# The opening of a fused linear-attention and tanh-shrink kernel: lam as eight numbers, other load queues, another order of the first steps

## The chip, the cores and the metric

The kernel runs on one core of a Trainium2 chip. The metric is the device time of one execution in microseconds (us). Beside it stand the times of one profiled execution and its trace.

## The reference

Two stages follow each other. The first is a linear attention with decay over 4 batches, 8 heads, 768 positions and 64 columns per head. The reference goes through blocks of 64 positions:

```python
pos = np.arange(block)
rel = pos[:, None] - pos[None, :]
Dmask = np.where(rel >= 0, lam[:, None, None] ** rel[None, :, :], 0.0)
lam_pow = lam[:, None, None] ** (pos[None, :, None] + 1)
for b in range(nb):
    intra = np.einsum('bhic,bhjc->bhij', qb, kb) * Dmask[None]
    intra = np.einsum('bhij,bhjd->bhid', intra, vb)
    inter = np.einsum('bhid,bhde->bhie', qb * lam_pow[None], kv_state)
    out[:, :, sl] = intra + inter
    kb_dec = kb * (lam[:, None, None] ** (block - 1 - pos[None, :, None]))[None]
    kv_state = lam_block[None, :, None, None] * kv_state + np.einsum('bhsd,bhse->bhde', kb_dec, vb)
```

`lam` holds eight numbers, one for each head. The output, seen as 3072 tokens of 512 numbers, goes into the second stage: `h = x @ w_in` (512 x 2048), `g = h - tanh(h)`, and `g @ w_out` (2048 x 512). `w_in` and `w_out` come as 64-bit floats, seen as 64-bit integers; q, k, v and lam are 32-bit floats.

## The kernel before

The positions are cut into 6 groups of 128, and one group of all 4 batches is 512 tokens. Group 0 is done with plain products; later groups use products of sums (a Strassen-like scheme), which the change does not touch. A chunk is one of q, k or v for one group and one batch: 128 positions x 8 heads x 64 columns, 256 KB, in pieces of 256 bytes.

**The opening steps of group 0.** For each batch b:

- `att_transpose(0, (b,))`: 4 transposes of q and 4 of k on TensorE into PSUM tiles `tp` (L384), each group of four copied out by ScalarE to `qt` and `kt` (L386).
- `att_scores(0, (b,))`: 8 products `sp` (L400), then two VectorE multiplications with the decay table `whole` (L407) to `ss`.
- `att_decay(0, b)`: VectorE multiplies the k chunk by the last column of the table (L430).
- `first_out(b)`: 8 products `op` of v and `ss` (L451). Two batches share a pair of PSUM banks; `first_tokens(half)` copies them to the tokens `xt` by ScalarE (L458).
- `kv_products(0, (b, b+1))`: 16 products `kv` of k and v for two batches (L439); `first_state` copies the result out (L463).

The decay table is made by `scans`: 8 VectorE scans (L110), one for each head, that multiply step by step by that head's lam. They read `lam_all`, a tile of 128 rows that all hold the eight lams, and the identity matrix `ident`, which GpSimd makes. Before, one DMA from GpSimd's queue fills `lam_all` with 128 copies of the eight numbers (L96).

**The plain products of unit 0.** `up_plain(0, ...)` is a generator: each `steps(unit, n)` takes n of its steps. One step is two products `h` (L895) of one block row i of `w_in` with a token tile. The first eight steps are for columns 11 and 21 (the first two batches), the next eight for 12 and 22. At the end of a column ScalarE takes the tanh (L900) and VectorE the difference (L901).

**The weights.** A block of `w_in` is 128 rows x 512 columns, 512 KB as it comes. `load_weights` loads blocks into four buffers `raw64` (WAHEAD = 4) and `weights(n)` rounds blocks until n are done: three ScalarE passes (L332 to L334) and two VectorE passes (L336, L337). Before, the first 16 blocks are all loaded from SP's queue (L260); blocks 2 and 3 of a unit come as two DMAs of 64 rows each (L250).

**What sets the order.** A scheduler orders the instructions on each engine; those given to `keep_in_program_order` (in group 0 nearly all of the opening) stay in the order of the text. `held(op, engines)` makes the next load that each named queue issues wait for `op`. The queues: SP (`nc.sync`) takes q chunks and w_in blocks; ScalarE's queue takes the k chunks of batches 0 and 1; GpSimd's (POOL's) takes v of group 0 and k of batches 2 and 3. An engine's queue issues in order, so a load that waits holds up all behind it.

**Idle products.** `idle_products(n)` puts n products of a tile of zeros into an unused bank (L361); they compute nothing that is read. Eight of them come first, as soon as VectorE has set the zeros (L95).

The text from L966 on lists the opening in order. After it `powers()`, group 1's attention, the other units and the sums follow in the same way as after the change.

Of the kernel before, what the change touches and what calls it, by code (L numbers as in the profile page):

```python
# [9 lines left out]
F32 = mybir.dt.float32  # L10
# [8 lines left out]
BLK = 128  # L19
# [5 lines left out]
def kernel(  # L25
# [32 lines left out]
    nc = tc.nc  # L58
    B, H, S, D = q.shape
# [33 lines left out]
    lam_all = const.tile([128, H], F32)  # L93
    fwd = const.tile([128, NP, BLK], F32)
    nc.vector.memset(fwd[:, 0, :], 0.0)  # L95
    nc.gpsimd.dma_start(out=lam_all, in_=bass.AP(tensor=lam.tensor, offset=lam.offset, ap=[[0, 128], [1, H]]))  # L96
    make_identity(nc, ident)

# [3 lines left out]
    whole = xpool.tile([128, 3, 2, HB], F32, name="whole", tag="tt").rearrange("s a b c -> s (a b c)")[:, 0:2 * DM].rearrange(  # L104
        "s (j p i) -> s j p i", j=2, p=NP)
    def scans(ps, ones):
        for j in range(2):
            for p in ps:
                h = 2 * p + j
                tc.keep_in_program_order(nc.vector.tensor_tensor_scan(  # L110
                    out=whole[:, j, p, :], data0=lam_all[:, h:h + 1].to_broadcast([128, BLK]), data1=ones, initial=0.0,
                    op0=AL.mult, op1=AL.add))


    scans(range(NP), ident)

    def masks():
        pin = tc.keep_in_program_order
# [20 lines left out]
    def tied(yes, op):  # L139
        return tc.keep_in_program_order(op) if yes else op  # L140
# [12 lines left out]
    def load_natural(g, b, names):  # L153
        for name, src, bufs in (("q", q, 2), ("k", k, 3), ("v", v, 4)):
            if name in names:
                if (g, b, name) in ((0, 2, "q"), (0, 3, "q"), (0, 3, "k")):
                    x = opool.tile([128, H, D], F32, name=f"{name}_nat", tag="o")
                else:
                    x = (qpool if name == "q" else io).tile([128, H, D], F32, name=f"{name}_nat", tag=name, bufs=bufs)
                rows = src[b, :, ts(g, BLK), :].rearrange("h s d -> s h d")  # L160
                if name == "q":
                    parts = [(nc.sync, x, rows)]
                elif g == 0:
                    parts = [(nc.scalar if name == "k" and b < 2 else nc.gpsimd, x, rows)]
                else:
                    parts = [(nc.sync, x[ts(1 - t, HALF), 4:8], rows[ts(t, HALF), 4:8]) for t in range(2)]
                    parts.insert(0, (nc.sync, x[:, 0:4], rows[:, 0:4]))
                for eng, to, of in parts:
                    op = tc.keep_in_program_order(eng.dma_start(out=to, in_=of))  # L169
                    if begin.get(eng) is not None:  # L170
                        wait_for(op, begin.pop(eng))
                raw[g, b][name] = x
# [67 lines left out]
    def load_block(eng, dst, kind, n, m, first=False):  # L240

        if kind == "out":
            tied(first, eng.dma_start(out=dst, in_=moe_w_out[ts(m * KH + n, 128), :].rearrange("k (a n) -> k a n", a=2)))
        elif m < 2:
            op = tied(first, eng.dma_start(out=dst, in_=w_in_u[ts(m, 128), :, ts(n, 256)]))
            if begin.get(eng) is not None:
                wait_for(op, begin.pop(eng))
        else:
            for j in range(2):
                op = tied(first, eng.dma_start(out=dst[ts(1 - j, 64)], in_=w_in_u[ts(2 * m + j, 64), :, ts(n, 256)]))  # L250
                if begin.get(eng) is not None:
                    wait_for(op, begin.pop(eng))

    def load_weights(n):

        while ready["loaded"] < min(n, ready["may"]):
            if moe_w_in.dtype != F32:
                raw64 = stage.tile([128, 2, 256], I64, name="raw64", tag="raw64", bufs=WAHEAD)
                block = blocks[ready["loaded"]]
                load_block(nc.gpsimd if ready["loaded"] in range(NU * KI, NU * KI + 4) else nc.sync, raw64, *block, True)  # L260
                wraw[ready["loaded"]] = raw64
            ready["loaded"] += 1

# [75 lines left out]
    def bank(name, tag, bufs):  # L339
        return psum.tile([128, 512], F32, name=name, tag=tag, bufs=bufs)  # L340


    for b in range(B):
        raw[0, b] = {}
    for b in (0, 1):
        load_natural(0, b, "qk")
    ready["may"] = 1
    load_weights(1)
    for b in (0, 1):
        load_natural(0, b, "v")  # L350
    ready["may"] = 2
    load_weights(2)
    at["loaded"] = B


    idle = bank("idle", "w", 1)

    def idle_products(n, first=False):

        for _ in range(n):  # L360
            tied(not first, nc.tensor.matmul(out=idle[:, 0:128], lhsT=fwd[:, 0, :], rhs=fwd[:, 0, :], start=True, stop=True))  # L361

    idle_products(8, True)


    state = const.tile([128, B, NP, D], F32)
# [4 lines left out]
    def att_transpose(g, bs):  # L371
        for b in bs:
            load(g * B + b + 1)
            t = raw[g, b]
            qt = work.tile([128, NP, BLK], F32, name="qt", tag="qt")
            kt = work.tile([128, NP, BLK], F32, name="kt", tag="kt")
            for dst, x in ((qt, "q"), (kt, "k")):
                if g >= GB:
                    tc.keep_in_program_order(nc.vector.transpose(out=dst.rearrange("d p i -> d (p i)"),
                                                                 in_=t[x + "b"].rearrange("d p r a -> d (p r a)")))  # L380
                else:
                    tp = bank("tp", "att", 4).rearrange("d (p s) -> d p s", p=NP)
                    for p in range(NP):
                        tied(g == 0 or p == 0, nc.tensor.transpose(out=tp[:, p, :], in_=t[x][:, 2 * p:2 * p + 2, :],  # L384
                                                                   identity=ident))
                    tied(g == 0, nc.scalar.activation(dst, tp, AF.Copy))  # L386
            qd = None
            if g > 0:
                qd = work.tile([128, NP, BLK], F32, name="qd", tag="qd")
                nc.vector.tensor_tensor(qd, qt, fwd, op=AL.mult)  # L390
            tr[g, b] = (qt, kt, qd)
# [36 lines left out]
    def att_decay(g, b):  # L428
        kp = raw[g, b]["k"].rearrange("s (p j) d -> s p j d", j=2)
        return tied(g != 1, nc.vector.tensor_tensor(kp, kp, bwd if g > 0 else bwd_first, op=AL.mult))  # L430
# [13 lines left out]
    def first_out(b):  # L444
        n, half = b % 2, b // 2
        if n == 0:
            reads[0, half] = [bank("op", "att", 4).rearrange("d (p b s) -> d p b s", p=2, b=2) for _ in range(2)]
        ops, ss, vn = reads[0, half], sc.pop((0, b)), raw[0, b]["v"]
        for p in range(NP):
            for j in range(2):  # L450
                tied(True, nc.tensor.matmul(out=out_dst(ops, n, p, j), lhsT=vn[:, 2 * p + j, :], rhs=ss[:, j, p, :],  # L451
                                            start=n == 0 and p % 2 == 0, stop=n == 1 and p % 2 == 1,
                                            skip_group_check=True))
# [502 lines left out]
    def steps(it, n):  # L956
        for _ in range(n):
            next(it)


    def held(op, *engines):
        begin.clear()
        begin.update({eng: op for eng in engines})

    def more_raw(n):
        ready["may"] = n  # L966
        load_weights(n)

    att_transpose(0, (0,))
    idle_products(3)  # L970
    held(att_scores(0, (0,)), nc.sync, nc.gpsimd)
    load_natural(0, 2, "qk")
    att_decay(0, 0)
    att_transpose(0, (1,))
    idle_products(2)
    first_out(0)
    att_decay(0, 1)
    held(att_scores(0, (1,)), nc.sync)
    more_raw(3)
    kv = kv_products(0, (0, 1))  # L980
    idle_products(2)
    weights(1)
    first_out(1)
    held(first_tokens(0)[0], nc.sync, nc.gpsimd)
    load_natural(0, 3, "qk")
    load_natural(0, 2, "v")
    more_raw(4)
    load_natural(0, 3, "v")
    ready["may"] = len(blocks)
    idle_products(6)  # L990
    unit = up_plain(0, [(i, c + 10 * a) for c in (11, 12) for i in range(KI) for a in range(2)])
    steps(unit, 2)
    weights(2)
    idle_products(4)
    att_transpose(0, (2,))
    steps(unit, 2)
    weights(3)
    att_scores(0, (2,))
    att_decay(0, 2)
    idle_products(6)  # L1000
    att_transpose(0, (3,))
    steps(unit, 2)
    weights(4)
    att_scores(0, (3,))
    first_out(2)
    att_decay(0, 3)
    idle_products(4)
    first_out(3)
    first_tokens(1)
    first_state((0, 1), kv)  # L1010
    steps(unit, 2)
    weights(5)
    steps(unit, 4)
    first_state((2, 3), kv_products(0, (2, 3)))
    weights(6)
    every(unit)
    weights(2 * KI)
# [177 lines left out]
```

## Time and profile before

| what | value |
|---|---|
| median of 3 runs | 657.41 us (657.17 to 658.46) |
| the profiled execution's own time | 657.46 us |
| its span (first to last instruction) | 655.7 us |
| TensorE (PE) busy | 649.3 us, 99% |
| VectorE (DVE) busy | 470.2 us, 72% |
| ScalarE (ACT) busy | 244.3 us, 37% |
| GpSimd (POOL) busy | 206.0 us, 31% |
| granted TensorE clock | 1.00 |

A row of a timeline gives the start and length in us from the span's start, the engine, the line of the kernel, the operation, the tiles written and read, the shape, and how many records were merged. A product of 32-bit floats is two matmul records. In square brackets stands the time for which the engine had been idle, and what ended that idle time. Records of TensorE overlap, so a row's length can reach past the next row's start. A DMA row's length is the time of issuing, not of the transfer. POOLq, SPq and ACTq are the queues' sequencers; in the views of DMA queues, q1 is SP's queue, q10 ScalarE's and q0 POOL's, with packets, MB, and the time of the packets as a share of the 16 DMA engines in that window.

### The profile page before, as it was taken

The numbers are of one execution on the slowest core, as the hardware profiler recorded it, in microseconds if no ns is written. First come the engines' busy times: TensorE is split into PE (matmuls) and PEld (weight loads), VectorE is DVE, ScalarE is ACT, GpSimd is POOL, SyncE is SP. The second block draws the span as 40 slices with busy tenths as digits, with TensorE's granted clock in tenths as the row PEclk, the third lists the DMA queues.
The fourth block names the chain that finished last, engine by engine and source line by source line (L and its number), as shares of the span: only waits on it lengthen the run. The fifth ranks groups of instructions, "written<-read, shape, count | busy, mean of one in ns | idle before, by whom it ended". The sixth has DMA issues, their size and how long they took to land.

```text
span 655.7 us, 14869 instructions
## 1 busy us (share of the span) xinstructions
PE 649.3 (99%) x5782; PEld 595.9 (91%) x5782; DVE 470.2 (72%) x893; ACT 244.3 (37%) x485; POOL 206.0 (31%) x354
## 2 busy tenths in 40 slices
PE   8999999999999999999999999999999999999998
PEld 7888888888888999988999988999988899998897
DVE  4447989968878895678786668788468697466663
ACT  3576964622321223532223442213453223263210
POOL 2100125776133334202335302243411254400241
PEclk9999999999999999999999999999999999999999
DMA  7939977997858768957656967576867476621374
GB/s 194 246 113 214 240 227 209 387 277 222 183 129 218 219 190 246 217 103 184 198 182 219 240 127 161 149 235 196 208 158 153 123 259 219 228 69 33 85 250 163
DMA packets 154422, 125.78 MB, mean 192 GB/s; under 512 B 124928, under 2 KB 127232, under 8 KB 154352
## 3 DMA queue, kind: packets, MB, share of 16 engines
q0 software_dynamic: 27072, 88.04, 43.3%
q1 hardware_dynamic: 125200, 36.27, 25.6%
q8 instruction: 46, 0.75, 0.5%
q10 hardware_dynamic: 2080, 0.52, 0.4%
q14 instruction: 24, 0.20, 0.1%
HBM read 103.81 MB, written 20.97 MB: 190 GB/s over the span
## 4 chain that ended last, share of the span: by engine, by line
PE 80%; DMA 6%; issue 5%; SPq 4%; DVE 3%; POOL 1%; ACT 0%; POOLq 0%; DVEq 0%
PE y L601 14%; PE y L839 12%; PE zw L839 9%; PE h L895 7%; PE y L685 5%; PE z L601 5%; PE acc L925 4%; PE y L786 4%; PE w L786 4%; PE z L685 3%; SPq L181 2%; DMA q_blk<-in_q_dram 2%; SPq L169 2%; PE w L685 1%; PE sp L418 1%
## 5 line engine op out<-in xcount | busy, mean ns | idle before, releaser
L744 POOL DMA_DIRECT2D wb<-fine x148 | 79.9, 540 | 186.3 <-PE y L786 69.6
L843 ACT ACTIVATE q<-y 128x128 f32<-128x128 f32 x96 | 26.7, 278 | 142.8 <-PE y L839 141.9
L839 PE MATMUL y<-wb,g 128*128 128x128 f32 x456 | 60.2, 277 | 0.0
L895 PE MATMUL h<-xt,w 128*128 128x256 f32 x256 | 58.2, 383 | 0.3 <-DVE w L337 0.3
L839 PEld LDWEIGHTS y<-wb,g 128*128 128x128 f32 x456 | 55.1, 192 | 0.6
L895 PEld LDWEIGHTS h<-xt,w 128*128 128x128 f32 x256 | 47.4, 190 | 7.8 <-DVE w L337 1.3
L747 POOL DMA_DIRECT2D wb<-factors x44 | 23.7, 541 | 84.3 <-PE y L786 50.8
L609 ACT ACTIVATE th<-g 128x512 f32<-128x512 f32 x40 | 25.2, 630 | 66.5 <-DVE g L627 50.7
L601 PE MATMUL y<-xt,w 128*128 128x256 f32 x192 | 45.0, 379 | 0.0
L610 DVE TENSOR_TENSOR g<-g,th 128x512 f32<-128x512 f32 x40 | 27.6, 691 | 20.7 <-ACT th L609 20.7
L601 PEld LDWEIGHTS y<-xt,w 128*128 128x128 f32 x192 | 36.4, 190 | 5.1 <-ACT g L618 0.2
L839 PE MATMUL zw<-wb,g 128*128 128x128 f32 x304 | 40.3, 276 | 0.3 <-DMA wb<-fine 0.3
L601 PE MATMUL y<-tt,ws 128*128 128x256 f32 x160 | 37.8, 379 | 0.0
L601 PE MATMUL y<-tt,w 128*128 128x256 f32 x160 | 37.8, 379 | 0.0
L601 PE MATMUL z<-xt,ws 128*128 128x256 f32 x160 | 37.8, 379 | 0.0
L839 PEld LDWEIGHTS zw<-wb,g 128*128 128x128 f32 x304 | 37.0, 192 | 0.7 <-DVE tt L666 0.5
L786 PE MATMUL y<-wb,g 128*128 128x256 f32 x160 | 37.3, 379 | 0.0
L786 PE MATMUL w<-wb,g 128*128 128x256 f32 x160 | 35.3, 379 | 0.0
L786 PEld LDWEIGHTS y<-wb,g 128*128 128x128 f32 x160 | 30.4, 190 | 4.1
L786 PEld LDWEIGHTS w<-wb,g 128*128 128x128 f32 x160 | 30.4, 190 | 4.1
L601 PEld LDWEIGHTS z<-xt,ws 128*128 128x128 f32 x160 | 30.4, 190 | 4.1
L601 PEld LDWEIGHTS y<-tt,w 128*128 128x128 f32 x160 | 30.3, 190 | 4.2
(212 smaller groups left out, 1465.7 us busy)
## 6 DMA issues: line engine op xcount, KB each, us to landing
wb<-fine POOLq DMA_DIRECT2D x148, 256.0 KB, 3.6
wb<-factors POOLq DMA_DIRECT2D x44, 256.0 KB, 4.9
wb<-fine_in POOLq DMA_DIRECT2D x36, 256.0 KB, 4.1
raw<-in_moe_w_out_dram SPq DMA_DIRECT2D x12, 512.0 KB, 5.0
rest<-fine POOLq DMA_DIRECT2D x20, 256.0 KB, 4.3
raw<-in_moe_w_in_dram SPq DMA_DIRECT2D x8, 512.0 KB, 7.2
raw<-in_moe_w_in_dram SPq DMA_DIRECT2D x16, 256.0 KB, 6.2
fine<-f POOLq DMA_DIRECT2D x16, 256.0 KB, 4.8
```

The lines of the kernel that those rows point to most:

```text
L169: op = tc.keep_in_program_order(eng.dma_start(out=to, in_=of))
L601: nc.tensor.matmul(out=t[:, m, :], lhsT=wt[:, kt, ts(m, 128)], rhs=x[:, kt, :], start=first and m == 0 and kt == 0, stop=kt == 1, skip_gro ...
L609: nc.scalar.activation(th, src, AF.Tanh)
L610: nc.vector.tensor_tensor(dst(c), src, th, op=AL.subtract)
L685: nc.tensor.matmul(out=dst[:, ts(u, 128)], lhsT=a, rhs=b, start=x in (1, 2, 5) and u == 0, stop=True, skip_group_check=True)
L744: nc.gpsimd.dma_start(out=t.rearrange("p m c -> p (m c)"), in_=fine[TWICE.index(n_), SUB.index(x_)].rearrange("p u c -> p (u c)"))
L747: nc.gpsimd.dma_start(out=t, in_=factors[XAT[FACT[n_][1]]][:, 2 * x_:2 * x_ + 2, :])
L786: nc.tensor.matmul(out=t[:, m, :], lhsT=a[:, u, kt, ts(m, 128)], rhs=wb[:, kt, :], start=first and u == 0 and m == 0 and kt == 0, stop=u = ...
L839: tied(x == STEPS[-1], nc.tensor.matmul(out=dst, lhsT=a[:, u, :], rhs=wb[:, ts(u, 128)], start=x in (1, 2) and u == 0, stop=u == NU - 1, s ...
L843: nc.scalar.activation(keep, dst, AF.Copy)
L895: tied(u == 0, nc.tensor.matmul(out=hm[c][:, m, :], lhsT=w1[u][:, i, a, ts(m, 128)], rhs=xt[0, t][:, i, :], start=m == 0 and i == 0, stop= ...
L925: nc.tensor.matmul(out=acc[n][:, r, :], lhsT=a[:, ts(r, 128)], rhs=b, start=kt == 0 and r == 0, stop=kt == KH - 1, skip_group_check=True)
```

## The change

- lam is loaded as eight numbers in eight rows (`few`), spread by VectorE to 8 x 128, turned by one small TensorE transpose (`rows`) and copied by VectorE to `lam_all`. The first 8 idle products and this transpose now stand ahead of all other TensorE work.
- v chunks of batches 0 and 1 move from POOL's queue to SP's. The first w_in block moves from SP's queue to POOL's, where it waits for the first scan. k of batch 2 follows it there; v of batch 2 and all of batch 3's k and v follow, held until the first batch's scores.
- q chunks of batches 2 and 3 and w_in blocks 1 to 3 are issued on SP without holds.
- batch 1's transposes and scores come ahead of batch 0's outputs, batch 2's transposes ahead of the first step of `h`; the state products of batches 0 and 1 come later, and the outputs of batches 2 and 3 come between steps of `h`.
- after the first eight, 16 idle products stand where there were 27.

```diff
--- before.py
+++ after.py
@@ -93,8 +93,18 @@
     lam_all = const.tile([128, H], F32)
     fwd = const.tile([128, NP, BLK], F32)
     nc.vector.memset(fwd[:, 0, :], 0.0)
-    nc.gpsimd.dma_start(out=lam_all, in_=bass.AP(tensor=lam.tensor, offset=lam.offset, ap=[[0, 128], [1, H]]))
+    few = const.tile([H, 1], F32, name="few")
+    nc.gpsimd.dma_start(out=few, in_=bass.AP(tensor=lam.tensor, offset=lam.offset, ap=[[1, H], [1, 1]]))
     make_identity(nc, ident)
+
+    idle = psum.tile([128, 512], F32, name="idle", tag="w", bufs=1)
+
+    def idle_products(n, first=False):
+
+        for _ in range(n):
+            op = nc.tensor.matmul(out=idle[:, 0:128], lhsT=fwd[:, 0, :], rhs=fwd[:, 0, :], start=True, stop=True)
+            if not first:
+                tc.keep_in_program_order(op)
 
 
 
@@ -104,15 +114,26 @@
     whole = xpool.tile([128, 3, 2, HB], F32, name="whole", tag="tt").rearrange("s a b c -> s (a b c)")[:, 0:2 * DM].rearrange(
         "s (j p i) -> s j p i", j=2, p=NP)
     def scans(ps, ones):
+        first = None
         for j in range(2):
             for p in ps:
                 h = 2 * p + j
-                tc.keep_in_program_order(nc.vector.tensor_tensor_scan(
+                op = tc.keep_in_program_order(nc.vector.tensor_tensor_scan(
                     out=whole[:, j, p, :], data0=lam_all[:, h:h + 1].to_broadcast([128, BLK]), data1=ones, initial=0.0,
                     op0=AL.mult, op1=AL.add))
-
-
-    scans(range(NP), ident)
+                first = first or op
+        return first
+
+
+    few_wide = xpool.tile([H, BLK], F32, name="few_wide", tag="xt1")
+    tc.keep_in_program_order(nc.vector.tensor_copy(few_wide, few.to_broadcast([H, BLK])))
+    rows = psum.tile([128, 512], F32, name="rows", tag="z", bufs=1)[:, 0:H]
+    idle_products(8, True)
+    tc.keep_in_program_order(nc.tensor.transpose(out=rows, in_=few_wide, identity=ident[0:H, 0:H]))
+    tc.keep_in_program_order(nc.vector.tensor_copy(lam_all, rows))
+
+
+    begun = scans(range(NP), ident)
 
     def masks():
         pin = tc.keep_in_program_order
@@ -161,7 +182,7 @@
                 if name == "q":
                     parts = [(nc.sync, x, rows)]
                 elif g == 0:
-                    parts = [(nc.scalar if name == "k" and b < 2 else nc.gpsimd, x, rows)]
+                    parts = [(nc.gpsimd if b > 1 else nc.scalar if name == "k" else nc.sync, x, rows)]
                 else:
                     parts = [(nc.sync, x[ts(1 - t, HALF), 4:8], rows[ts(t, HALF), 4:8]) for t in range(2)]
                     parts.insert(0, (nc.sync, x[:, 0:4], rows[:, 0:4]))
@@ -257,7 +278,7 @@
             if moe_w_in.dtype != F32:
                 raw64 = stage.tile([128, 2, 256], I64, name="raw64", tag="raw64", bufs=WAHEAD)
                 block = blocks[ready["loaded"]]
-                load_block(nc.gpsimd if ready["loaded"] in range(NU * KI, NU * KI + 4) else nc.sync, raw64, *block, True)
+                load_block(nc.gpsimd if ready["loaded"] in (0, *range(NU * KI, NU * KI + 4)) else nc.sync, raw64, *block, True)
                 wraw[ready["loaded"]] = raw64
             ready["loaded"] += 1
 
@@ -342,25 +363,12 @@
 
     for b in range(B):
         raw[0, b] = {}
-    for b in (0, 1):
-        load_natural(0, b, "qk")
-    ready["may"] = 1
-    load_weights(1)
-    for b in (0, 1):
-        load_natural(0, b, "v")
-    ready["may"] = 2
-    load_weights(2)
+    for names in ("qk", "v"):
+        for b in (0, 1):
+            load_natural(0, b, names)
     at["loaded"] = B
 
 
-    idle = bank("idle", "w", 1)
-
-    def idle_products(n, first=False):
-
-        for _ in range(n):
-            tied(not first, nc.tensor.matmul(out=idle[:, 0:128], lhsT=fwd[:, 0, :], rhs=fwd[:, 0, :], start=True, stop=True))
-
-    idle_products(8, True)
 
 
     state = const.tile([128, B, NP, D], F32)
@@ -966,52 +974,54 @@
         ready["may"] = n
         load_weights(n)
 
+    held(begun, nc.gpsimd)
+    more_raw(1)
+    more_raw(2)
+    load_natural(0, 2, "q")
+    more_raw(3)
+    load_natural(0, 2, "k")
     att_transpose(0, (0,))
-    idle_products(3)
-    held(att_scores(0, (0,)), nc.sync, nc.gpsimd)
-    load_natural(0, 2, "qk")
+    idle_products(4)
+    held(att_scores(0, (0,)), nc.gpsimd)
+    load_natural(0, 2, "v")
+    load_natural(0, 3, "qkv")
+    more_raw(4)
+    ready["may"] = len(blocks)
     att_decay(0, 0)
+    idle_products(1)
     att_transpose(0, (1,))
+    idle_products(4)
+    att_scores(0, (1,))
+    first_out(0)
+    weights(1)
+    att_decay(0, 1)
+    idle_products(5)
+    first_out(1)
+    first_tokens(0)
     idle_products(2)
-    first_out(0)
-    att_decay(0, 1)
-    held(att_scores(0, (1,)), nc.sync)
-    more_raw(3)
-    kv = kv_products(0, (0, 1))
-    idle_products(2)
-    weights(1)
-    first_out(1)
-    held(first_tokens(0)[0], nc.sync, nc.gpsimd)
-    load_natural(0, 3, "qk")
-    load_natural(0, 2, "v")
-    more_raw(4)
-    load_natural(0, 3, "v")
-    ready["may"] = len(blocks)
-    idle_products(6)
+    att_transpose(0, (2,))
+    weights(2)
     unit = up_plain(0, [(i, c + 10 * a) for c in (11, 12) for i in range(KI) for a in range(2)])
     steps(unit, 2)
-    weights(2)
-    idle_products(4)
-    att_transpose(0, (2,))
-    steps(unit, 2)
+    att_scores(0, (2,))
+    kv = kv_products(0, (0, 1))
     weights(3)
-    att_scores(0, (2,))
     att_decay(0, 2)
-    idle_products(6)
     att_transpose(0, (3,))
     steps(unit, 2)
+    first_out(2)
     weights(4)
     att_scores(0, (3,))
-    first_out(2)
     att_decay(0, 3)
-    idle_products(4)
+    steps(unit, 2)
     first_out(3)
     first_tokens(1)
     first_state((0, 1), kv)
     steps(unit, 2)
     weights(5)
-    steps(unit, 4)
+    steps(unit, 2)
     first_state((2, 3), kv_products(0, (2, 3)))
+    steps(unit, 2)
     weights(6)
     every(unit)
     weights(2 * KI)
```

## The prediction, made before the run

> **What bounds the kernel now.** I read the page first, then the timeline of each engine over the first 60 us, the DMA view in short windows, and the chain of waits. The page says that TensorE is the bound:
>
> ```profile
> PE 649.3 (99%) x5782; PEld 595.9 (91%) x5782; DVE 470.2 (72%) x893; ACT 244.3 (37%) x485; POOL 206.0 (31%) x354
> ```
>
> PE is idle for 655.7 - 649.3 = 6.4 us. But some of its "busy" time is idle products, which compute nothing. The timeline of PE (start, length, line, tile, records, idle before) shows where both lie:
>
> ```profile
> 1.06 3.78 PE L361 MATMUL idle<-fwd 128*128 128x128 f32 x16 [1.06 <-DVE fwd L95]
> 4.63 1.08 PE L384 MATMUL tp<-ident,q_nat 128*128 128x128 f32 x4
> ...
> 11.36 1.09 PE L451 MATMUL op<-ss,v_nat 128*64 128x128 f32 x16 [0.67 <-DMA v_nat<-in_v_dram]
> ...
> 16.22 1.60 PE L361 MATMUL idle<-fwd 128*128 128x128 f32 x12
> 17.66 1.89 PE L895 MATMUL h<-xt,w 128*128 128x256 f32 x8
> ...
> 32.44 5.45 PE L895 MATMUL h<-xt,w 128*128 128x256 f32 x24
> ```
>
> Two records make one product, and one h step too is two products. From 32.44 on PE is dense (its only wait up to 60 us is 0.26 us). Everything the change touches lies before that, so I measure it at one mark: the start of the second half of unit 0 (columns 12 and 22), 8 records into the last row, at 32.44 + 1.73 = 34.2 us. What is gained at this mark is gained at the end if nothing later is late.
>
> The two things that came late were lam and v:
>
> ```profile
> 7.09 2.63 DVE L110 TENSOR_TENSOR_SCAN whole<-lam_all,ident 128x128 f32<-128x128 f32 x8 [6.08 <-DMA lam_all<-in_lam_dram]
> 9.64 1.26 DVE L407 TENSOR_TENSOR ss<-sp,whole 128x512 f32<-128x512 f32 x2
> ```
>
> lam was issued at 1.25 and landed 5.7 us later, at 6.95; scans, first scores and first outputs queue behind it. v's first chunk, issued by POOL at 2.44, landed 8.8 us later, at 11.2. The DMA view shows why: by windows of half a microsecond, POOL's queue (q0) moved nothing at 7.0 to 7.5 (first two rows) and 20 packets at 8.0 to 8.5 (last row), though v had been issued by 4.25:
>
> ```profile
> q1 hardware_dynamic: 108, 0.13, 87.2%
> q10 hardware_dynamic: 87, 0.02, 19.5%
> ...
> q0 software_dynamic: 20, 0.08, 41.3%
> ```
>
> While SP's and ACT's queues hold small-packet chunks of q and k, POOL's queue hardly moves; beside the large packets of w_in it gets about half.
>
> **Step prices, from the rows (warm).** Eight transposes of one batch (tp) 0.88 (20.28 to 21.16), scores (sp) 1.09, outputs (op) 1.02, state products of two batches (kv) 1.08, two h steps 1.73, an idle product 0.24 (1.44 us for 6). Work up to the mark: 4 tp + 4 sp + 4 op + kv + 8 h steps = 3.5 + 4.4 + 4.1 + 1.1 + 6.9 = 20.0. So 34.2 - 20.0 = 14.2 us of the opening are waits, idle products, and slow clock.
>
> **Idle products.** The first 8 stay. After them there were 3+2+2+6+4+6+4 = 27, now 4+1+4+5+2 = 16: 11 x 0.24 = 2.6 us of PE less. This is only gain where the operands are there.
>
> **lam.** The DMA of 128 rows becomes one of 8 numbers; added are a DVE copy (8x128, at most the memset's 0.17), one small transpose on PE (a record, about 0.2 to 0.4) and a DVE copy of 128x8 (about 0.1): 0.5 us from landing to the next PE step, 0.8 to the first scan. The new cost is that the small transpose stands in PE's order *ahead of* the first q transposes. These began at 4.63; now they begin at s = landing + 0.5, and everything on PE is queued behind that wait. No row shows an 8-number DMA from POOL; bounds are 4.9 (POOL's packets of lam first moved in the window 4.0 to 4.5, plus receipt) and 7.5 (lam's own 6.95 and some more). I take 6.2: nearest to lam, as the queues ahead are the same (q, k on SP and ACT, same issue times), with less to write and read. So s = 6.7. That is 2.1 us of PE lost at the front, while the scans run from 7.0 to 9.7, as before.
>
> **Clock.** The first products ran at 3.57 / 16 = 0.22 us a record against 0.12 later, and PE was fast only from about 6.7 on, 5.6 us after its first product. Now PE stands idle from 4.84 to 6.7, so I price tp and the 4 idle products behind it as slow ones: tp 1.73 (4.63 to 6.36) for 0.88, and 8 records x 0.22 = 1.78 for 0.96, together 1.65 more, over 3.5 us. Bounds: nothing if the clock holds; 1.65 + (5.6 - 3.5) / 2 = 2.7 if the rise takes as long as the first one did. I take 1.65, the middle. [...]
>
> **The PE order after.** From s: tp0 0.88, 4 idle 0.96, sp0 1.09, 1 idle 0.24, tp1 0.88, 4 idle 0.96, sp1 1.09, op0 1.02, 5 idle 1.20, op1 1.02, 2 idle 0.48, tp2 0.88: 10.7 to the first h step, or 12.35 with the slow clock. Then h, sp2, kv, tp3, h, op2, sp3, h, op3, h = 6.9 + 6.2 = 13.1 to the mark. With s = 6.7: first h at 19.05 (it was 17.66, with kv ahead of it and tp2 behind), mark at 32.15: all 16 idle products now lie ahead of the first h, and the 14 that lay behind it (3.4 us) are gone. **Gain 34.2 - 32.15 = 2.05 us.**
>
> What must hide under it: qt and kt on ACT need 1.75 us after tp starts (25.51 to 27.23), and tp + 4 idles cover 1.84. Scores of batch 0 (DVE 1.26) end at about 12.8, op0 starts at 14.5; batch 1's end near 16, op1 starts at 16.7. kv leaves its place ahead of op1, where the state copy on ACT did not need it yet.
>
> **Loads.** v0 and v1 move from POOL's queue to SP's, behind q1: six chunks of 256 KB at some 250 GB/s from 2 us on land by about 9 (were 11.2 and 12.5). Block 0 of w_in moves from SP to POOL and waits for the first scan (7.8); POOL has nothing else to do, but k2 stands behind it there, now without a hold of its own. First packets at about 9.5, half of the rate: v0 and v1 took 4.4 us from 8.0 on, so block 0 lands at 14.5, k2 at 17. ACT's three passes (2.0) and DVE's two end by 17.5, before 19.05; tp2 at 18.2 finds k2. q2, block 1, 2, q3, 3 run on SP without holds, so SP has issued them early; v2 waits for batch 0's scores, k3 and v3 queue behind it: 5.2 MB in all at 245 GB/s are in by 23 to 24, and v3 is read at 28, block 3 by ACT near 25. I cost the moved loads at nothing; this cover is 1 us at k2 and 1.5 at block 0, and beyond it each microsecond of delay costs one.
>
> **The sum.** The profiled execution took 657.46 with a span of 655.7, 0.05 above the median of the runs. 657.46 - 2.05 gives **655.4 us**. No change here is what a measurement cannot tell, about 0.2%, 1.3 us.
>
> **Rivals.**
> *The eight numbers land no sooner* (6.95 to 7.5): s = 7.45 to 8.0, mark 32.9 to 33.45, gain 0.75 to 1.3: 656.2 to 656.7. For it: the queues ahead are unchanged and what delays POOL's packets is other packets. [...]
>
> *They land early* (4.9): s = 5.4, the clock rises as before, so only some 0.75 of the slow price is paid; first h at 16.85, mark at 30.0, gain 4.2, less a microsecond if block 0 and k2 then come late: 653.2 to 654.2. For it: lam's first packets moved by 4.5.
>
> *Slower: POOL's queue starves.* SP's unheld stream (v0, v1, blocks 1 to 3, q2, q3: 2.3 MB left at 8 us) keeps the engines busy for 9.4 us more. If POOL's queue is served only behind it, block 0 lands near 20.5, is rounded at 23.3, and the mark is 36.4: 2.2 later, 659.7. It decides from a landing of 18 us on. For it, the window at 7 us above; against it, POOL moved about as many bytes as SP beside w_in's packets from 8 us on, and only q2 and q3 in that stream are small-packet chunks.
>
> *The gain is eaten later.* The one wait for weights up to 60 us (0.26 us) is for a w_in block that queued behind q's loads of the next group, as the chain that ended last shows (start, length, what):
>
> ```profile
> 38.97 9.89 PE h L895 x44
> 48.86 0.54 SPq L169
> ...
> 53.81 3.35 DMA q_nat<-in_q_dram
> ...
> 59.90 4.25 PE h L895 x18
> ```
>
> If this chain kept its time, the mark's gain would end there: 657.4. Against it: SP's loads there wait for buffers that ACT frees in an order tied to PE's h steps, so they come earlier with PE.
>
> **Chances.** Forecast 0.42, early 0.18, no sooner 0.17, eaten 0.09, starved 0.14. Forecast and early give nearly all of "faster" (0.60); no sooner, eaten and the weak end of the forecast "same" (0.26); starved "slower" (0.14). The range goes from the early case, 653.2, to a delay of POOL's loads that turns the sum by 2.8 us, 658.2; full starvation is left out.
>
> **What would show it.** Right: few landing near 6.2, PE idle from 4.84 to about 6.7 with the rows transpose at its end, slow records behind it, first h near 19, the mark near 32.2, idle products down by 22 records. Wrong: h waiting for DVE w (block 0) or tp for k_nat; op waiting for v_nat; a wait longer than 0.3 us for a weight near 58.

## The result: slower by 0.27%, and the profile after

The changed kernel takes 659.04 us (median of 11 runs, 658.06 to 661.89), the kernel before 657.49 beside it; the ratio is 1.0027 (95% interval 1.0015 to 1.0038). The forecast was 655.4, in 653.2 to 658.2. The profiled execution took 660.13 with a span of 658.3. It is 1.1 us above the median of its kernel, so the two traces differ by more (2.6 us) than the medians do (1.6).

The page of after: TensorE's busy time fell by only 0.1 us, though 11 idle products (2.6 us by the prediction's price) are gone, so other products took longer; and its idle time grew from 6.4 to 9.1.

```profile
PE 649.2 (99%) x5761; PEld 595.1 (90%) x5761; DVE 471.1 (72%) x895; ACT 244.4 (37%) x485; POOL 204.9 (31%) x353
```

The timeline of PE in the opening of after:

```profile
6.94 0.24 PE L132 MATMUL rows<-ident,few_wide 8*128 8x8 f32 x1 [2.10 <-DVE few_wide L129]
7.11 1.11 PE L392 MATMUL tp<-ident,q_nat 128*128 128x128 f32 x4
...
8.87 1.91 PE L105 MATMUL idle<-fwd 128*128 128x128 f32 x8
10.71 2.08 PE L408 MATMUL sp<-qt,kt 64*128 64x128 f32 x16
12.72 0.49 PE L105 MATMUL idle<-fwd 128*128 128x128 f32 x2
...
20.78 1.89 PE L903 MATMUL h<-xt,w 128*128 128x256 f32 x8
...
26.77 0.63 PE L392 MATMUL tp<-ident,k_nat 128*128 128x128 f32 x4 [1.33 <-DMA k_nat<-in_k_dram]
...
34.12 2.21 PE L903 MATMUL h<-xt,w 128*128 128x256 f32 x9
```

The rows transpose stands at 6.94, the first scores take 2.08 (1.16 for 16 records later; the granted clock is up from 12.70), the first h step is at 20.78 instead of 19.05, and batch 3's k chunk holds PE for 1.33. The mark is 34.12 + 1.73 = 35.85: 1.7 us later than before, where 2.05 sooner was forecast.

That is not all. I laid the ScalarE instructions of the two traces beside each other, in order: after starts them 1.67 us late from 42 us to 335 (1.38 around 130), 3.05 late from 344 on, 2.5 to 2.7 late from 441 on. So a second loss of 1.38 us lies 310 us behind the last line that the change touches. The table of waits of PE (wait, us in total, times, longest), 60 to 655 us, first of after:

```profile
PE op L518 <- issue: 0.9, 1, 0.9
PE h L903 <- DVE w L358: 0.3, 1, 0.3
PE acc L933 <- DVE g L939: 0.2, 1, 0.2
```

and of before:

```profile
PE zw L839 <- DMA wb<-fine: 0.3, 1, 0.3
PE h L895 <- DVE w L337: 0.3, 1, 0.3
PE acc L925 <- DVE g L931: 0.2, 1, 0.2
```

The first line of after is new: in group 3's attention PE waits for nothing that the profile shows. In the timeline of PE it is at 345:

```profile
343.90 0.40 PE L518 MATMUL op<-ss,v_nat 128*64 128x64 f32 x8
345.21 0.92 PE L518 MATMUL op<-ss,v_nat 128*64 128x64 f32 x24 [0.90 <-issue]
```

GpSimd's queue does something else just ahead of it. Its timeline in after, where wb blocks of the later products are loaded:

```profile
332.31 0.54 POOL L752 DMA_DIRECT2D wb<-fine  x1 [3.93 <-PE y L847]
333.51 0.54 POOL L752 DMA_DIRECT2D wb<-fine  x1 [0.66 <-PE zw L847]
336.51 3.78 POOL L752 DMA_DIRECT2D wb<-fine  x7 [2.47 <-PE zw L847]
```

The same program lines in before:

```profile
331.83 0.54 POOL L744 DMA_DIRECT2D wb<-fine  x1 [0.66 <-PE zw L839]
332.73 0.54 POOL L744 DMA_DIRECT2D wb<-fine  x1 [0.36 <-PE y L839]
333.62 0.54 POOL L744 DMA_DIRECT2D wb<-fine  x1 [0.35 <-PE y L839]
```

Before issues a load each 0.89 us. After stops for 3.0 us from one issue to the next, and then sends seven without a pause, so that the transfers fall into 340 to 345 us, beside the attention's own work: by windows, 277 GB/s there against 111 before.

### The profile page after: what moved, and what is told of

The parts are those of the page before. It is cut to its first block, busy times and chain, and to the rows that moved or that the text cites. A ratio compares the mean times of both kernels' runs of the same rounds, so it can differ in the third digit from the quotient of the medians.

```text
span 658.3 us, 14826 instructions
## 1 busy us (share of the span) xinstructions
PE 649.2 (99%) x5761; PEld 595.1 (90%) x5761; DVE 471.1 (72%) x895; ACT 244.4 (37%) x485; POOL 204.9 (31%) x353
## 5 line engine op out<-in xcount | busy, mean ns | idle before, releaser
L851 ACT ACTIVATE q<-y 128x128 f32<-128x128 f32 x96 | 26.6, 277 | 142.8 <-PE y L847 141.8
L618 DVE TENSOR_TENSOR g<-g,th 128x512 f32<-128x512 f32 x40 | 27.6, 691 | 20.7 <-ACT th L617 20.7
```

The lines of the kernel that those rows point to most:

```text
L618: nc.vector.tensor_tensor(dst(c), src, th, op=AL.subtract)
L851: nc.scalar.activation(keep, dst, AF.Copy)
```

## The experiments

The edits are shown shortened. Theories at the start: **F**, the front (lam's wait and the slow clock) sets the loss; **Q**, k of batch 3 behind the held v of batch 2 on GpSimd's queue; **C**, TensorE's program is 21 records shorter, so the loads of its own code fall elsewhere against the work, and PE runs dry at one of them; **L**, the new loads cause both losses. "Mark" is the delay against before at 33 to 45 us, "gap" PE's issue wait in group 3's attention, both in the one profiled execution; the mark of one execution can differ by 1.6 us from that of another with the same opening (+0.28 in e1, +1.92 in e10).

**e1: k of batch 3 ahead of v of batch 2.**

```diff
     load_natural(0, 2, "k")
+    load_natural(0, 3, "k")
...
-    load_natural(0, 3, "qkv")
+    load_natural(0, 3, "qv")
```

> After, but k of batch 3 is issued on POOL's queue ahead of the held v of batch 2 (order: block 0, k2, k3, then v2, v3 behind the hold). Theory Q (POOL's queue: k3 stands behind v2, which waits for the first scores at 14.1 us, and lands at 26.6, so its transposes wait and the mark - start of the second half of unit 0 - is 1.6 us late): the transposes of batch 3 follow each other without a gap, mark 35.85 - 1.6 = 34.2, time 1.6 below after: about 657.4, ratio to before 1.000. Theory F (the front alone: PE waits for the turned lam until 7.1 and runs slow until 12.7; the queue has enough slack elsewhere): the gap at k3 only moves to another load (v2 or v3 for the outputs), mark 35.5 or later, 658.7 or more.

Ratio 1.0017 (1.0006 to 1.0028). Mark +0.28: the opening's loss is nearly gone, though PE now waits for the last q chunk (0.6). The gap stays, 0.6, within steps of +0.36 and +0.85 at 339 and 344. Q holds for the opening, not for the time. The clock rose sooner here (10.29) than in after (12.70); e9 and e12 below have e1's opening with a clock as late as after's (12.97, 12.90), and their marks are +0.25 and +0.24.

**e2: 13 idle products first instead of 8**, so that PE is busy until the numbers are there.

> After, but 13 idle products ahead of the turn of lam instead of 8, so that PE stays busy from 1.06 to about 7.0. Theory F with the clock as its main part: the clock is up at about 6.7 as in before, not at 12.7; transposes, idle products and scores of batch 0 take 2.9 us instead of 5.6, and the first h comes up to 1.6 us earlier (20.8 to 19.2, where block 0's rounding binds); the mark gains at least 1.5: about 657.4. Theory Q, or if the clock was not the matter: the first part is faster by 2.7 but k3 (queued behind v2) still ends the wait; v2's hold falls 2 us earlier, so the gain at the mark is 1 to 2 all the same: the trace must tell by the gap ahead of the k transposes of batch 3. If the clock does not rise earlier although PE is busy, nothing changes: 659.0.

Ratio 1.0036 (1.002 to 1.0052). The waits of PE from 4 to 36 us in e2:

```profile
PE tp L392 <- DMA q_nat<-in_q_dram: 2.2, 1, 2.2
PE tp L392 <- DMA k_nat<-in_k_dram: 1.3, 1, 1.3
```

The clock is up at 7.00, ahead of the first transposes, and the first scores end 2.6 us sooner than in after; 0.4 of that is left at the mark, +1.25, where I had expected 1.5 or more. The rest is waited away at these two chunks. Gap 1.1.

**e3: lam in 128 rows as before the change; e4: the turn behind the first transposes.**

```diff
-    few = const.tile([H, 1], F32, name="few")
-    nc.gpsimd.dma_start(out=few, ...)
+    nc.gpsimd.dma_start(out=lam_all, ...)      # e3; without few_wide, rows and their copies
...
+    att_transpose(0, (0,))                     # e4: ahead of the rows transpose
```

> After, but lam as before: one DMA of 128 rows, no turn on PE, no copies; loads, holds and order as after. Theory F: transposes of batch 0 start at 4.6, clock up at 6.7, scans at about 7.1; the first h is bound by block 0 (raw issue at 7.5 to 8.2, landing near 16): 19.2 at the latest against 20.8; v2's hold ends at 11 instead of 14, so k3 lands 2 to 3 us earlier; mark 32 to 33, time 655.3 to 656.5, ratio 0.997 to 0.9985. Theory Q: k3 still late by its queue: 657.5 or more.

> After with the eight numbers, but the turn on PE stands behind the transposes of batch 0 instead of ahead of them. Theory F: these start at 4.6, as in before, the turn runs at 6.9 as now, scans at 7.5; everything as in the run with lam in 128 rows but some 0.3 later: 655.6 to 656.8. Theory Q: 657.5 or more. The difference of this and the 128-row run is the price of the eight numbers by themselves: 0.0 to 0.4.

e3: 1.005 (1.0035 to 1.0066), mark +1.57, PE waits 4.1 us for q chunks and the clock is down from 25.0 to 28.5. e4: 1.0036 (1.002 to 1.0051), mark +3.48, waits of 2.3 for k and 2.6 for q, the clock down from 27.6 to 31.0. Gaps 1.3 and 1.1. Both are misses. In e3 the first h comes at 17.26, 3.5 us sooner than in after; the wait for the last q chunk and the slow clock behind it take that back. F does not hold by itself.

**e5: e1 with 10 idle products back (5 first, 5 ahead of batch 3's transposes); e6: before, with 11 idle products fewer.** Together they test C from both sides.

```diff
-    idle_products(6)       # before, in e6: 6, 4, 6, 4
+    idle_products(4)       # become 4, 0, 4, 1
```

> After with k3 issued early (as in the first run) and ten more idle products at places where PE only waits: five ahead of the turn of lam, five ahead of batch 3's transposes. PE's program then has 40 instructions more than after's, 2 fewer than before's. New theory C (PE's program comes in loads of 256 instructions, and the change, by taking 42 instructions out of the opening, moved a load boundary into the short products of group 3's attention, where PE ran dry at its instruction 6081 in all five kernels so far, for 0.6 to 1.35 us): that gap is gone, and the end lies only as far behind before as the mark does: mark 34.3 to 35.5, time 657.5 to 658.8, ratio 1.000 to 1.001, a microsecond below the same kernel without the ten. Rival L (the gap at group 3 comes of the loads being late or early, not of the place in the program): the gap stays at 0.6 or more near 344 us.

> Before with 11 of its idle products left out (6, 4, 6, 4 become 4, 0, 4, 1), so with 44 PE instructions fewer, nothing else changed. My forecast's step (11 x 0.24 = 2.6 us of PE gained): time 655 to 656. Theory D (the opening is bound by the bytes of its loads, about 5.2 MB, which come in at the same rate in every order tried, 4.9 to 5.2 MB by 24 us): the mark stays at 33.2 to 34.3 with waits in place of the idle products. Theory C on top of D: a gap of about 1 us appears at instruction 6081, near 344 us: 657.5 to 658.6, ratio 1.000 to 1.002.

e5: 1.0038 (1.0024 to 1.0051), mark +0.48, gap 1.1, with a PE program one record shorter than before's. e6: 1.0007 (0.999 to 1.0024), mark -0.20, no such gap, with one record less than after's. The length of the program, C's reason, falls; the wait for code comes back below. e6 also shows what 11 idle products less are worth: 0.2 us at the mark, and no gain in time. The waits of PE from 4 to 36 us in e6:

```profile
PE op L451 <- DVE k_nat L430: 1.4, 1, 1.4
PE op L451 <- DVE ss L407: 1.4, 2, 1.2
PE tp L384 <- DMA q_nat<-in_q_dram: 0.2, 1, 0.2
```

**e7: the changed kernel with the loads of before; e8: before with the new loads alone** (their queues, holds and order; PE's program as before).

> After with the loads and holds of before (v0 and v1 on POOL, blocks 0 and 1 on SP from the start, q2 and k2 held until the first scores, block 2 until the second, q3, k3, v2, block 3 until the first token copy); lam, order and idle products as after. The holds hang on steps that the front makes late (first scores at 12.8 instead of 9.6), so everything they hold comes late: mark 36 to 37.5, time 660 to 661.5, with the gap at instruction 6081. If instead loads were the whole loss at the mark: mark 34.3 or less, 658.5.

> Before with only the loads of after: v0 and v1 on SP's queue, block 0 on POOL's behind the first scan, no holds for q2, q3 and blocks 1 to 3, the same hold for v2, k3, v3. Lam, order of PE and idle products as before, so PE's program has the same length. Theory D with the order of the loads as the cause: q3 and k3 land at 24 to 26.5 instead of 21.8 and 23.8, transposes of batch 3 wait, mark 35.3 to 36.5; no gap at instruction 6081; ratio 1.0015 to 1.0035. If the loads are not the cause: mark 34.2 or earlier, ratio 0.998 to 1.0005.

e7 (one run, 660.14): mark +3.08 as expected, but without the gap that I expected. e8: 1.0034 (1.002 to 1.0048), mark +0.40, gap 2.0 within +2.7 at 339 to 345. For e8 I had expected a late mark and no gap; that the ratio lies in the range I gave is luck. The gap goes with the loads: in every kernel with the new ones so far, in none with the old ones. L holds for the second loss.

What could loads that ended at 35 us do at 333? GpSimd's queue had issued 6 transfers with 4360 rows in the opening of after, 7 with 6272 before (a row is one contiguous piece; a chunk has 1024). The stop in after is at transfer 168 (counted from 0), 2.1 us more than the same load takes in before. Such a stop is in before as well, at transfer 151, 1.8 us more than the same load takes in after, in a quiet stretch (timeline of POOL in before):

```profile
299.99 0.54 POOL L744 DMA_DIRECT2D rest<-fine  x1 [0.29 <-DMA k_blk<-in_k_dram]
302.30 0.54 POOL L744 DMA_DIRECT2D rest<-fine  x1 [1.76 <-issue]
```

The next one comes 100 transfers and 13,696 rows later, in both kernels, and takes 2.4 us more than the same load in the other one. So the place may be set by what the queue has issued.

**e9 and e10: e1 with idle rows on GpSimd's queue**, 1920 rows of 4 bytes in one transfer (e9), 8 rows in one transfer (e10), written over a dead q chunk.

```diff
+    last = first_tokens(1)[1]
+    pad = raw[0, 3]["q"]...[0:128, 0:30 step 2]      # e10: [0:8, 0:1]
+    wait_for(nc.gpsimd.dma_start(out=pad, in_=<lam, step 0>), last)
```

> e1 with one idle transfer on GpSimd's queue at about 33 us (1920 rows of 4 bytes, written over a q chunk that is dead): GpSimd's queue has then issued 7 transfers and 6280 rows after the opening, as before the change (7 and 6272), where the new loads leave 6 and 4360. What it looks at: in every kernel with the new loads GpSimd's load number 168 (a wb block, at 333 us) comes 3.0 us behind number 167, when all earlier ones have landed, and then seven follow at 0.53 us each; in kernels with the old loads it comes 0.9 us behind. Theory 'queue position' (this wait stands at a place that is set by what the queue issued in the opening): the wait is gone from 333 us, the burst of loads at 336 to 340 too, TensorE does not run dry in group 3's attention at 344 us, and the time is e1's less about 1.2 us, 658.1 or less. Theory 'opening' (the later loss is a later echo of what the opening delayed): all stays, 659.4.

> The same with an idle transfer of 8 rows: 7 transfers as before the change, but 4368 rows. If the number of transfers sets the place of the wait, the gap ahead of the load that was number 168 falls to 0.9 us and the time is about 658.1, as in e9. If the rows set it, the wait stays within one load of its place and the time is e1's, 659.4. If neither e9 nor e10 removes it, the queue's position is not the cause.

e10: 1.0024 (1.0007 to 1.0042); the stop is at the same load, one number on (169), and the gap is there, 1.1. Its mark is +1.92, in e1's opening, which gave +0.28: here PE waits 3.0 us for the last q chunk, which landed at 26.4 instead of 24.8. e9: the stop is back at transfer 151. The timeline of POOL in e9:

```profile
310.93 0.54 POOL L752 DMA_DIRECT2D rest<-fine  x1 [0.30 <-DMA k_blk<-in_k_dram]
313.23 0.54 POOL L752 DMA_DIRECT2D rest<-fine  x1 [1.76 <-issue]
```

From 317 to 420 us its delay does not change, and there is no gap. One transfer more does not move the stop to another load, its 1920 rows do. But e9 took 1.0185 (1.0145 to 1.0226): the rows filled the DMA engines from 34 to 50 us, and h waited for a weight. The windows of e9 (busy us, clock, DMA share, GB/s):

```profile
34.00:38.00 4.00, 4.00 (x47) 3.32 (x46) 2.41 (x4) 3.38 (x6) 0.95 (x1) 1.00 1.29 4
38.00:42.00 4.00, 4.00 (x20) 3.54 (x19) 1.12 (x2) 1.98 (x4) 0.00 (x0) 1.00 0.89 0
```

My expectation left the price of the rows out.

**e11: before with e6's idle products and ss3 sooner.** In e6 PE waits for ss (above) because VectorE rounds w_in block 3, the fourth, first. The timeline of VectorE in e6, where the scores end at 28.0:

```profile
29.29 0.69 DVE L337 CUSTOM_DVE_ANT_0 w<-w,r 128x1024 uint16<-128x1024 uint16 x1 [0.87 <-ACT r L334]
29.90 1.28 DVE L407 TENSOR_TENSOR ss<-sp,whole 128x512 f32<-128x512 f32 x2
```

```diff
-    weights(4)
     att_scores(0, (3,))
+    weights(4)
```

> The kernel before with its old loads, e6's 11 idle products fewer, and chunk 3's scores ahead of w_in block 4's rounding in the program, so that VectorE masks ss3 ahead of that block. In e6 chunk 3's scores end at 28.0 us and VectorE comes to ss3 at 29.9; here it can at 28.0. Theory 'order of VectorE' (in the opening before the change the last link is this masking, and not lam, the loads or the clock): the second half of unit 0 starts 1.6 to 1.8 us sooner than before the change, at 32.4 to 32.6 us, and the time is 1 to 1.8 us under the one before, 655.7 to 656.5. Theory 'loads' (the opening is bound by its bytes): something lands late instead and the start stays at 34.0 to 34.2, the time within 0.3 of before.

656.27 against 658.05: 0.9971 (0.9961 to 0.9981). It beats both kernels, with the old lam and the old loads. The timeline of PE in e11 has the row of h at 30.93 that began at 32.44 before; the delay at the mark is -1.64, 1.4 of it by the swap (e6 has -0.20):

```profile
28.33 1.09 PE L451 MATMUL op<-ss,v_nat 128*64 128x128 f32 x16
29.35 0.49 PE L361 MATMUL idle<-fwd 128*128 128x128 f32 x2
29.77 1.09 PE L451 MATMUL op<-ss,v_nat 128*64 128x128 f32 x16
30.93 5.23 PE L895 MATMUL h<-xt,w 128*128 128x256 f32 x23
```

In this trace 0.7 us is lost again between 144 and 241 us, and its end is 0.9 ahead of before's.

**e12 and e13: the 1920 rows at a quiet place** (about 278 us, to DRAM), on e1 and on the changed kernel itself.

```diff
+            if sent["n"] == 59:
+                wait_for(nc.gpsimd.dma_start(out=pad[:, :, 0:1], in_=ident[...]), op)
```

> e9's idle transfer (1920 rows of 4 bytes) at another place: e1, with the rows written to DRAM by GpSimd's queue behind the load at 286 us, ahead of a stretch in which that queue issues nothing for 8.6 us. In e9 the same rows stood in the way of the w_in blocks at 34 us and cost 10.9 us at once, and behind it no gap at 344 us followed. Theory 'queue position': here the rows cost under 0.3 us themselves, load number 168's wait of 3.0 us is gone from 333 us, no TensorE gap follows at 344 us, and the time falls from e1's 1.0017 of before to 0.999 to 1.001 (the start of unit 0's second half at +0.3 us, and -0.5 and +0.2 later as in the others). Theory 'delay' (in e9 the gap was missing because everything stood 11 us later, not because of the rows): the gap at 344 us stays, and the time is e1's, 1.0015 to 1.003.

> The changed kernel as it is, with e12's 1920 idle rows late on GpSimd's queue. It splits the change's own loss into its two places: the opening (+1.7 us at the start of unit 0's second half) and the gap behind GpSimd's 3.0 us wait (+1.4 us at 339 to 345 us). Theory 'two places': the opening keeps its +1.7, the wait and the gap are gone, -0.5 at 441 us and +0.2 at 541 us stay, so the profiled end is at +1.2 to +1.5 and the ratio falls from 1.0027 to about 1.0005 (0.9995 to 1.0015). Theory 'only the opening counts' (the gap is taken back elsewhere): the ratio stays at 1.002 to 1.003.

e12: 0.999 (0.9979 to 1.0002); its interval lies below e1's. The timeline of POOL in e12 goes on without a stop at 332; the stop is now at transfer 156, 3.56 us behind the issue before it, where before has 1.73 for the same load:

```profile
310.27 0.54 POOL L753 DMA_DIRECT2D wb<-fine  x1 [2.92 <-PE w L798]
313.83 1.06 POOL L753 DMA_DIRECT2D wb<-fine  x2 [3.02 <-PE w L798]
...
331.38 0.54 POOL L753 DMA_DIRECT2D wb<-fine  x1 [3.93 <-PE y L851]
332.58 0.54 POOL L753 DMA_DIRECT2D wb<-fine  x1 [0.67 <-PE zw L851]
333.47 0.54 POOL L753 DMA_DIRECT2D wb<-fine  x1 [0.36 <-PE y L851]
```

There is no gap at 344, and the delay is +0.75 from 229 to 420 us, then +0.22, and +0.7 at the end. e13: 1.001 (0.9996 to 1.0024), the stop moved and the gap gone there too. Its other half was a miss, so that the ratio lies in the range I gave is in part luck: the mark came at +0.35 instead of +1.7, in the same opening program. Its timeline of PE says why:

```profile
7.08 0.20 PE L132 MATMUL rows<-ident,few_wide 8*128 8x8 f32 x1 [2.24 <-DVE few_wide L129]
7.20 0.66 PE L392 MATMUL tp<-ident,q_nat 128*128 128x128 f32 x4
...
19.09 1.97 PE L907 MATMUL h<-xt,w 128*128 128x256 f32 x8
...
24.38 0.63 PE L392 MATMUL tp<-ident,q_nat 128*128 128x128 f32 x4 [1.15 <-DMA q_nat<-in_q_dram]
```

In this execution the clock stayed up over PE's idle time (2.24 us; the first scores took 1.16, in after 2.08) and the first h came at 19.09, as forecast; then the wait for the q chunk and others took back what the forecast had gained on before. Against after, 1.3 us of its sooner front is left at the mark: the hold of batch 3's k ended sooner too, and k landed at 24.6 instead of 26.6. So after's 1.67 needs both, the slow front and k behind the hold; with one of them gone it is 0.2 to 0.4 in e1, e9, e12 and e13, though not in e10. As its opening differed, e13 does not weigh the second loss in the changed kernel by itself; e1 against e12 does, 0.27%, about 1.8 us, where the steps at 339 and 344 in e1's trace make 1.2.

## Why the prediction was wrong

The profiled execution came 4.7 us behind the forecast: 3.7 at the mark, 1.0 behind it. Two steps failed in kind, the loads priced at nothing and the mark carried to the end; others were off in size.

- **lam.** The eight numbers landed at 6.55 (6.2 was taken) and PE began its transposes at 7.11 instead of 6.7: 0.4 late. 128 rows had landed at 6.95 before, but that difference is not made by the eight rows: with the new loads 128 rows landed at 6.35 (e3) and 6.52 (e8), eight at 6.36 to 6.69. So the rival "no sooner" had the better reason, as far as these landings show. The steps behind the landing were priced in part from no row: the copy of 128 x 8, put at about 0.1, took 0.17; from the landing to PE's next step it was 0.56 (0.5 was taken), to the first scan 0.94 (0.8).
- **Clock, priced 1.65 with bounds 0 and 2.7.** In the profiled run it was up only at 12.7, 5.6 us after the transposes began: transposes, idle products and scores took 5.6 us where the warm prices make 2.9, so the price was 2.7, the upper bound (the slow scores, 0.9, were not in the 1.65). The same front paid 2.7 in e7, e9 and e12, 1.5 to 1.6 in e1 and e10, and 0.1 in e13. The range was right; the price differs between executions with the same first steps.
- **From first h to mark, 13.1.** It was 15.07: 1.55 more at batch 3's k chunk, the rest in h steps that ran at 1.83 to 1.93 instead of 1.73 (before has 1.82 too where another product follows). With the 1.73 at first h (0.4 of lam, 1.0 of the clock, 0.3 in smaller steps) that makes the 3.7 by which the mark was missed.
- **"I cost the moved loads at nothing."** This is the step that failed in the opening. I took 245 GB/s and one landing for all. By windows, after moved 168 GB/s up to 8 us, 250 up to 16, 200 up to 24, with the DMA engines full from 8 us on (share 1.10). The last q chunk, issued at 9.8, landed at 22.3, and at 21.8 to 26.4 in the other kernels that issue it unheld; k of batch 3, held behind v on its queue, landed at 26.6, and PE waited 1.33 us for it. Wherever the front was quick (e2, e3, e13), q and k took all or part of it back (waits of 3.5, 4.1 and 1.5 us).
- **Idle products, "2.6 us of PE less".** They stood over waits. e6 takes 11 away for a gain of 0.2; PE waits for VectorE instead. What could be gained lay in VectorE's order: e11's swap brings 1.4 us more at the mark.
- **"What is gained at this mark is gained at the end."** This failed by the second loss: +1.4 us at 339 to 345, +0.2 at 541. Another -0.5 at 441 is no effect of the change: before's trace has a wait of 0.3 for a wb block there, and e6 and e7, with the old loads, gain the same 0.5 on it there. I looked at GpSimd's queue for the order of its loads only, not for what their rows do to its later stops.
- **The rivals.** The slower one named the right suspects, the moved loads, but the wrong place: block 0 landed at 16.6, under its limit of 18. That its 659.7 lies near the measured time is luck.

Why PE runs dry at 345 us can be read from the loads of TensorE's code. Among its DMA records (kind instruction) the trace of after has 46 of them, 16 KB each, for 11,793 instructions (weight loads and waits counted), so some 256 instructions a load. The gap is at the same instruction, number 6081, in all eight kernels that have it, whatever the work is there. The last code load ahead of it starts when PE is at instruction 5967 to 6062 in these eight, and at 5800 to 5866 in the seven without a gap. In after it starts at 342.92, and PE goes on at 345.21; in the eight, PE goes on 2.3 to 2.6 us after that start, and the gap is 0.63 us where the load starts at 5967 and 1.98 where it starts at 6062. Counted on from 6081 in steps of 256, no first instruction of a load starts sooner than 2.29 us behind its load in any of the fifteen traces. So PE waits there for its own code. What stays open is why this load starts late. The runs show that it comes with the burst of wb loads and goes with it; that the burst delays the code is not shown.

## What to carry to other kernels

A change of loads in the opening can move a stop of GpSimd's queue hundreds of microseconds later (here from the load issued at 302.3 us before to the one at 336.5 after): compare the two traces instruction by instruction to the end, and look at the issue times of each queue where they part. Before moving loads forward, add up bytes and the landing of the *last* chunk that each step needs; before taking a wait away at the front, ask what stands at the far end, here a masking of 1.3 us behind a rounding on VectorE, mended by swapping two lines (with e6's idle products gone; the swap alone was not run). An idle product taken away is a gain only if the operands of the work behind it are there: 11 fewer in e6 gained 0.2 us at the mark, where 2.6 had been priced.

## What the runs showed of the hardware

**A stop of GpSimd's queue.** In each trace two transfers are issued late, by an amount that hardly changes with the kernel: 1.8 us at transfer 151 and 2.4 at 251 (before, e6, e7, e9, e11), 2.1 at 168 and 2.4 at 268 (after and the other kernels with the new loads; 169 and 269 in e10), 1.8 at 156 and 2.4 at 255 (e12, e13). It is not a wait until all earlier transfers have landed: in before transfer 151 is issued at 302.30, and the two ahead of it land at 302.89 and 304.34. From the first to the second stop the queue issues 100 transfers with 13,696 rows, in e12 and e13 99 with 13,568. What sets this distance is not shown.

**The price of small rows.** 1920 rows of 4 bytes hold the DMA engines from 34 to 50 us in e9 (4, 0, 0 and 10 GB/s by windows of 4 us), and delay the kernel by 10.9 us at 144 us; the same number behind the load of 273 us costs nothing that e12's trace shows.

**Steps of the granted clock.** In e10 the granted clock rises at 4.70, falls at 8.11 and rises again at 11.53, 3.41 us apart. Its windows:

```profile
4.70:8.11 3.41, 1.43 (x13) 1.31 (x13) 1.17 (x5) 0.48 (x1) 0.06 (x1) 1.00 1.36 217
8.11:11.50 3.39, 3.39 (x25) 2.94 (x23) 1.84 (x6) 0.60 (x2) 2.50 (x3) 0.50 1.10 246
```

PE was busy for 1.43 of the 3.41 us ahead of the fall; in e13 it was busy for 1.81 from 5.48 to 8.89, and the clock stayed up. The same first steps had their clock up at 12.7 (after), 10.3 (e1), 12.9 (e12), or from 5.5 on without a fall (e13): the time of the rise differs between executions. Behind an idle stretch of 2.10 us at the front, the first steps of after took 2.7 us more than the warm prices; in e13, behind 2.24, they took 0.1 more. The changed kernel's runs spread over 3.8 us, before's over 1.8; that this comes of the clock is not shown.

**A queue that stood still.** From 17.5 to 21.0 us in after, GpSimd's queue (q0), to which three chunks had been issued from 14.4 to 17.0, moved 2 packets while SP's (q1) moved 1176 of q's small pieces and w_in:

```profile
q1 hardware_dynamic: 1176, 0.65, 118.3%
q0 software_dynamic: 2, 0.00, 0.1%
```
